# Column tiles for every product, and residual rows added by VectorE, in a recurrent-memory attention kernel

## The chip, the core and the metric

The kernel runs on one core of a Trainium2 chip, as one launch. The metric is device time in microseconds. The kernel before takes 1845.33 us (median of three runs, 1842.41 to 1847.87). Five engines work beside each other, each from its own in-order stream: TensorE (PE; the profile lists its weight loads apart, as PEld), VectorE (DVE), ScalarE (ACT), GpSimd (POOL) and SyncE (SP, which only issues DMAs here). Products are written to PSUM[...].

## What is computed

A sequence of 2048 rows of width 512 goes through two kinds of layer in turn, A, B, A, B, each with a layer norm ahead and a residual add behind.

```python
def _A_ref(x, mem0, Wq, Wk, Wv, Wo, seg_len):       # 32 heads of 128, memory of 8 rows, segments of 32
    mask = (idx[:, None] < M) | (idx[:, None] >= idx[None, :])
    mem = mem0
    for s in range(n_seg):                          # 64 segments, one after the other
        h = jnp.concatenate([mem, xs], axis=1)      # 8 + 32 rows
        q, k, v = h @ Wq, h @ Wk, h @ Wv            # (einsum per head)
        scores = where(mask, q @ k.T * scale, -1e9)
        o = softmax(scores) @ v @ Wo
        mem = o[:, :M, :].copy()                    # memory of the next segment
        outs.append(o[:, M:, :])
# B: linear attention over all rows, 32 heads of 16
    pq, pk = phi(q), phi(k)                         # phi(t) = t+1 if t>0 else exp(t), + 1e-6
    kv = sum over rows of pk x v;  z = sum of pk
    o = (pq @ kv) / (pq @ z + 1e-6) @ wo
x = x + A(layernorm(x)); x = x + B(layernorm(x))    # twice
```

Layer A is a recurrence: the projections of a segment need the memory rows that the segment before made.

## The kernel before

The kernel is written as a list of operations with what each reads and writes. A list scheduler in the kernel's own source puts them in one fixed order per engine, from rough costs and tuned priorities, and emits that with the semaphore waits that it needs.

```python
# priority of an operation: its step and a tuned offset of its name and number
nd.prio = -(step * PERIOD + OFFSET[name][k])
# on PE, the scheduler prefers to stay in the mode ("col" or "full") of the product before,
# unless another one is more urgent by MODE_SLACK
```

A segment has 40 rows. The block of 32 columns that the kernel projects as "block" holds the 8 memory rows and the first 24 rows of the segment; the remaining 8 rows of four segments ("left" rows; they don't depend on the memory for q, k and v) are projected together, once for each group G of four segments.

Projections use column tiles: four products, each with 32 stationary columns, write to the four groups of 32 PSUM partitions.

```python
for j in range(4):                                                   # L789
    r = pe.matmul(tl.f32()[32 * j:32 * j + 32, 0:512], blk[:, c, :], W[:, c, o:o + 512],
                  start=(c == 0), stop=(c == 3), tile_position=(0, 32 * j))
```

q and k are then turned, by a DMA transpose or by PE (L811), as two flags say for each half b of the heads:

```python
QDMA = (True, False)
KDMA = (True, False)
```

The memory's attention uses the whole array, with 128 stationary columns:

```python
def mm(pe, a, kk):                                                   # mem_attention
    for i, hh in enumerate(hhs):
        o = 128 * a + 32 * i
        r = pe.matmul(tl.f32()[:, o:o + 32], kk[:, hh, :, :].rearrange("p j x -> p (j x)"),   # L873
                      qT[:, r2, hh, :, 0:8], start=True, stop=True)
    return r
# once with kTl (left keys), once with kT; exp (L880); mask (L882, 128x256)
... sums: one_sb x Pm (L890, whole array); ln, exp; vimg/vleft x Pm (L903, L904, whole array)
```

The input rows have score products of their own, in column tiles, once the left queries have been copied over the memory's columns of qT:

```python
for b in range(2):                                                   # x_attention
    evac(qT[:, r2, hs, :, 0:8], qTl[:, g2, hs, :, gl], 128, ...)
    for hh in range(4 * b, 4 * b + 4):
        for j in range(4):
            r = pe.matmul(tl.f32()[32 * j:32 * j + 32, 32 * hh:32 * hh + 32], kT[:, r2, hh, j, :],   # L928
                          qT[:, r2, hh, j, :], start=True, stop=True, tile_position=(0, 32 * j))
... exp (L932), mask (L934), sums (L944, L947), scaling (L956, L958),
    vimg/vleft x Pbx (L971, L972, whole array, 128 and 32 columns)
```

The output projection (L999, column tiles) leaves its two halves on partitions 0 to 63 and 64 to 127. Copies (L609 on ACT, L610 on DVE) bring it to `outW` in 32-bit form. From there `next_mem` (L1024) makes the next memory, and for the residual a selector product sums the two halves and puts the rows in their place in a PSUM tile that is kept for four segments:

```python
def pick(pe, tl, sel, u, first, last):
    for d in range(2):
        r = pe.matmul(tl.f32()[:, 256 * d:256 * d + 256], sel(d), outW[:, u, :],              # L1041, f32r
                      start=first and d == 0, stop=last, skip_group_check=True)
# after four segments and their left rows:
add("dve", lambda v: v.tensor_tensor(x, x, tl.f32()[:, :], ALU.add), ...)                     # L1061
```

Layer B's products (L1151, L1163, L1169, L1187, L1212, L1259, L1269) and the transposes of the layer norm (L762) use the whole array. `x_move` is a DMA that GpSimd issues.

Of the kernel before, what the change touches and what calls it, by code (L numbers as in the profile page):

```python
# [6 lines left out]
F32 = mybir.dt.float32  # L7
# [12 lines left out]
MODE_SLACK = 29.57  # L20

LOOK = 0.055
# [3 lines left out]
    "ld0": (6.40,),  # L26
    "ld1": (5.00,),
    "ld2": (7.30,),
    "ld3": (-7.35,),
    "ld4": (-7.70,),  # L30
    "startF": (-6.70,),
    "prepF": (-2.85, 0.10, -2.70, 11.90, -1.50, -3.10, -1.60, 3.50, 2.40, 5.50, -13.60),
    "left0F": (0.00, 3.20, -5.50, 3.25, -0.15, 1.65, 3.95, -0.70),
    "left1F": (7.50, -11.05, 2.90, 13.75, 0.55, 0.50, 0.60, -3.30),
    "leftv0F": (-18.35, -9.35),
    "leftv1F": (-3.35, 0.00),
    "leftsF": (-2.60, 3.10, -0.60, 1.10),
    "warm": (2000.00,),
    "xlF": (7.05,),
    "qk0F": (-1.55, -16.30, 17.30, -1.50, -2.05, -2.55, -1.15, -1.55),  # L40
    "qk1F": (6.30, 1.10, -2.90, -0.20, 4.80, -6.90, 12.05, -10.25),
    "v0F": (-7.30, -21.15),
    "v1F": (33.10, -4.10),
    "mem0F": (3.95, -0.55, -1.40, -2.60, -33.00, 21.50, -6.90, -14.80, -1.80),
    "mem1F": (-1.60, 1.55, -2.50, -16.95, 7.80, -12.35, 1.60, -0.70, -1.90),
    "outF": (31.15, -14.85, 5.15, -3.10),
    "nextF": (-0.10, -1.35, -1.25),
    "xF": (-0.85, 21.45, 3.55, -11.80, -20.85, -15.05, 6.45, -1.40, 4.05, 0.30, -9.80, -5.60, -0.40, 0.95,
        1.45, 9.50, 1.00, -8.30, 8.15, 0.25, -4.40, -0.30, 0.30),
    "qk0": (-23.70, 0.00, 0.80, -6.15, 1.50, 2.10),  # L50
    "qk1": (2.90, 1.80, -13.45, 4.95, 1.10, 6.10, -0.00, -5.35),
    "v0": (1.95, -0.20),
    "v1": (10.85, -3.90),
    "mem0": (-15.05, -20.45, -14.25, -22.45, 3.65, -9.20, -4.75, 5.00, 1.60),
    "mem1": (10.75, -4.70, -1.35, -1.75, -42.80, 0.00, 11.70, -10.95, -10.30),
    "out": (-8.45, -7.05, -8.75, 2.10),
    "next": (-1.00, 6.50, -14.75),
    "res": (44.95, 1.15, -1.05, 2.95, 1.15, -20.45, -3.70),
    "x": (-2.10, 0.00, -3.10, -8.00, 2.15, -12.80, 15.20, 3.00, -3.15, -4.80, -4.50, 3.05, -0.75, -9.50, -0.40,
        0.00, -1.20, 0.05, 2.05, 4.40, 35.75, 5.95, -12.85),  # L60
    "prep": (-0.40, 0.80, 0.90, 0.75, 5.05, 11.85, 5.20, -6.20, -1.90, 12.15, -3.75),
    "left0": (-0.50, 3.85, -5.00, -2.55, -3.35, 0.30),
    "left1": (-5.30, -12.45, -0.35, -5.85, -0.70, -2.25),
    "leftv0": (39.05, 6.60),
    "leftv1": (29.85, -6.05),
    "lefts": (-7.25, 1.75, 2.50, -1.30),
    "xl": (-3.15,),
    "bi": (11.00, -1.30, -0.45, 5.25, 4.85, 6.95, -7.45, -4.85, 0.20, -18.85, -4.90, 15.35, 25.85, 0.00, 41.05,
        7.15, -0.05, -7.85, 9.60, 1.30, -1.40, 0.30, 1.25),
    "qk0L": (-16.00, 5.55, 0.60, 3.20, -1.85, -0.85, 0.10, -0.25),  # L70
    "qk1L": (-5.50, -13.55, 1.75, 1.70, -1.30, -7.25, -8.55, -2.55),
    "xL": (-0.05, -1.75, 1.75, -1.05, 4.00, 8.30, -10.35, -20.40, 3.70, 5.75, -1.75, 2.35, 1.20, -8.20, -1.65,
        4.15, -5.85, -1.65, 6.05, 0.15, -2.40),
    "lr": (-3.85, -4.35, 5.15, -13.85, -8.30, -5.75),
    "outL": (-2.55, 0.20, 1.15, 3.70),
    "resL": (-7.00, 4.00),
    "biL": (-7.30, 5.95, 1.10, -1.30, -6.60, 2.00, -0.05, 0.00, 0.00, -17.45, 2.45, 7.50, 16.85, -6.25, -3.20,
        -19.15, 19.00, 31.50, 0.25, 2.05, -0.05, -31.10, -0.35),
    "bm": (5.90, -7.40, 0.50, -3.90, 5.00, -7.20, 8.75, -4.70, 1.50, 12.25, -0.80, 20.40, 7.75),
    "boF": (0.75, 4.90, 0.00, 18.95, 10.55, 29.80, 5.70, 5.50),  # L80
    "bo": (6.95, -0.40, -16.65, -1.90, 4.25, -14.80, 4.90, 0.00),
    "ldL": (-21.30, -4.95),
    "boL": (-2.85, -30.50, 4.55, 3.30, -8.15, -12.55, 15.70),
    "boZ": (-10.55, -8.10, -4.05, 12.50, 1.95, 0.00, -4.80),
# [11 lines left out]
def c_pe4(n_mm, n):  # L96
    return n_mm / 4.0 * max(0.0255, (n / 2.4 + 3.0) * 1e-3)


def c_pe(n_mm, n):  # L100
    return n_mm * max(0.0255, (n / 2.4 + 3.0) * 1e-3)
# [24 lines left out]
class _Prog:  # L126
# [27 lines left out]
    def add(self, engs, fn, cost, reads=(), writes=(), tiles=(), dsem=None, urgent=False, mode="full",  # L154
# [337 lines left out]
def _build_kernel(nc, A_x, A_mem0, A_Wq, A_Wk, A_Wv, A_Wo, A_seg_len, B_wqkv, B_wo, out):  # L492
# [13 lines left out]
    QDMA = (True, False)  # L506
    KDMA = (True, False)
# [26 lines left out]
    selx_sb = sb("selx_sb", [128, 2, 224], F32R)  # L534
    sell_sb = sb("sell_sb", [128, 2, 128], F32R)
    selz_sb = sb("selz_sb", [128, 2, 128], F32R)
    outW = sb("outW_sb", [128, 3, 256], F32R)
    maskbd_sb = sb("maskbd_sb", [128, 128])
    epsb_sb = sb("epsb_sb", [128, 1], F32)
    eps6_sb = sb("eps6_sb", [128, 1], F32)  # L540
    memT0_sb = sb("memT0_sb", [128, 4, M])
    st_sb = sb("st_sb", [128, 2, 16], F32)


    ARENA_N = 34320
    arena = sb("arena_sb", [128, ARENA_N])
    off = [0]

# [782 lines left out]
```

The softmax here doesn't subtract the row's maximum and nothing guards it: scores larger than these inputs give would overflow.

## Time and profile before

The profiled execution lasts 1841.2 us.

| quantity | value |
|---|---|
| time, median of 3 | 1845.33 us |
| DVE busy | 1091.8 us (59%) |
| ACT busy | 1168.1 us (63%) |
| POOL busy | 76.9 us (4%) |
| mean granted TensorE clock | 0.992 |
| DMA transposes | 368, 2.9 us to landing |
| projections L789, PE busy (q, k, v) | 346.6, 318.3, 361.6 us |
| output projection L999, PE busy | 311.6 us |
| selector products L1041, PE busy | 61.4, 15.9 and 1.0 us |

How to read it: a group's busy time is the union of its instructions' times. Matmuls overlap, so the mean duration of one (381 ns for a 512-column product) is longer than the time from its start to the next start; the spacing of starts is what PE spends. In a group's line, after the bar, stand busy us and mean ns, then the idle time of the engine just before these instructions and what ended it. A shape such as 128*32 128x512 is the stationary operand (contraction by columns) and the moving one. In a line of waits stand us in total, how many, and the longest.

### The profile page before, as it was taken

How to read it: one execution, taken by the hardware profiler on the slowest of the kernel's cores; microseconds unless marked ns; L12 is line 12 of the kernel's file. 1: busy time of each engine (PE TensorE's matmuls, PEld its weight loads, DVE VectorE, ACT ScalarE, POOL GpSimd, SP SyncE). 2: the span in 40 equal slices, each digit the busy share in tenths (PEclk: the TensorE clock that was granted, in tenths of full speed). 3: DMA queues.
4: the chain of work that ended last, by engine and by line, in shares of the span. 5: the costliest groups of instructions: out<-in, count | busy, mean ns of one | idle time of the engine just before them, and what ended most of it. 6: DMA issues, size and time to landing. Idle time of an engine off the chain costs nothing.

```text
span 1841.2 us, 100785 instructions
## 1 busy us (share of the span) xinstructions
PE 1763.0 (96%) x46707; PEld 1199.6 (65%) x46707; DVE 1091.8 (59%) x3259; ACT 1168.1 (63%) x3036; POOL 76.9 (4%) x182
## 2 busy tenths in 40 slices
PE   5999999999999999999799999999999999999997
PEld 2566666666666766676566666666766766666663
DVE  2356655655666566666555655666656566666666
ACT  3566666666666666666466666666667666666664
POOL 3000000000000000000000000000000000000000
PEclk9999999999999999999899999999999999999999
DMA  9322122212222121212012222222122222122222
GB/s 366 86 35 43 38 40 38 47 38 44 38 38 41 38 46 38 42 39 41 19 26 38 40 38 49 38 41 46 38 40 47 41 43 41 41 43 48 45 74 87
DMA packets 218933, 94.85 MB, mean 52 GB/s; under 512 B 202536, under 2 KB 212656, under 8 KB 216976
## 3 DMA queue, kind: packets, MB, share of 16 engines
q1 hardware_dynamic: 211312, 60.22, 18.0%
q0 software_dynamic: 5616, 15.60, 2.9%
q10 hardware_dynamic: 1584, 12.58, 1.7%
q8 instruction: 365, 5.98, 1.4%
q14 instruction: 56, 0.46, 0.1%
HBM read 29.63 MB, written 10.49 MB: 22 GB/s over the span
## 4 chain that ended last, share of the span: by engine, by line
PE 83%; DMA 11%; ACT 3%; DVE 2%; issue 1%; SPq 0%; ACTq 0%; DVEq 0%
PE pb L789 37%; PE pb L999 16%; DMA arena_sb<-arena_sb 9%; PE pb L873 4%; PE pb L971 3%; PE pb L811 3%; PE pb L1151 3%; PE pb L1041 3%; PE pb L928 2%; PE pb L890 2%; PE pb L1187 1%; ACT arena_sb L609 1%; DMA Wk_sb<-in_A_Wk_dram 1%; PE pb L904 1%; PE pb L903 1%
## 5 line engine op out<-in xcount | busy, mean ns | idle before, releaser
L609 ACT ACTIVATE arena_sb<-pb 128x512 bf16<-128x512 f32 (+6 forms) x1365 | 674.0, 504 | 375.5 <-PE pb L789 327.8
L610 DVE CAST arena_sb<-pb 128x512 bf16<-128x512 f32 (+3 forms) x438 | 207.8, 475 | 354.3 <-PE pb L789 157.6
L789 PE MATMUL pb<-Wv_sb,arena_sb 128*32 128x512 bf16 x5120 | 361.6, 381 | 0.1
L789 PE MATMUL pb<-Wq_sb,arena_sb 128*32 128x512 bf16 x5120 | 346.6, 383 | 1.3 <-ACT arena_sb L609 0.7
L789 PE MATMUL pb<-Wk_sb,arena_sb 128*32 128x512 bf16 x5120 | 318.3, 381 | 5.5 <-DMA Wk_sb<-in_A_Wk_dram 5.5
L999 PE MATMUL pb<-Wo_sb,arena_sb 128*32 128x256 bf16 x10368 | 311.6, 274 | 4.9 <-issue 3.3
L999 PEld LDWEIGHTS pb<-Wo_sb,arena_sb 128*32 128x32 bf16 x10368 | 269.0, 97 | 16.2 <-issue 5.1
L956 DVE TENSOR_TENSOR arena_sb<-arena_sb 32x256 bf16<-32x256 bf16 x512 | 213.2, 416 | 108.6 <-ACT arena_sb L952 95.6
L789 PEld LDWEIGHTS pb<-Wk_sb,arena_sb 128*32 128x32 bf16 x5120 | 139.6, 97 | 136.5 <-DMA Wk_sb<-in_A_Wk_dram 5.7
L789 PEld LDWEIGHTS pb<-Wq_sb,arena_sb 128*32 128x32 bf16 x5120 | 134.2, 97 | 108.5 <-DVE arena_sb L610 8.8
L789 PEld LDWEIGHTS pb<-Wv_sb,arena_sb 128*32 128x32 bf16 x5120 | 136.8, 97 | 94.1 <-issue 2.8
L609 ACT ACTIVATE outW_sb<-pb 128x128 fp32r<-128x128 f32 x233 | 64.6, 277 | 171.5 <-PE pb L999 148.8
L610 DVE COPY arena_sb<-pb 128x512 bf16<-128x512 bf16 (+2 forms) x295 | 112.3, 396 | 68.6 <-PE pb L811 64.9
L971 PE MATMUL pb<-arena_sb 128*128 128x128 bf16 x1024 | 127.9, 216 | 0.0
L958 DVE TENSOR_TENSOR arena_sb<-arena_sb 32x64 bf16<-32x64 bf16 x512 | 110.8, 216 | 15.9
L873 PE MATMUL pb<-arena_sb 128*128 128x32 bf16 x2016 | 104.1, 178 | 12.4 <-DMA arena_sb<-arena_sb 11.0
L972 PE MATMUL pb<-arena_sb 128*128 128x32 bf16 x1024 | 115.0, 177 | 0.0
L880 ACT ACTIVATE arena_sb<-pb 128x256 bf16<-128x256 f32 x252 | 95.8, 381 | 27.7 <-PE pb L873 26.6
L811 PEld LDWEIGHTS pb<-id_sb,arena_sb 128*32 128x32 bf16 x4352 | 70.4, 97 | 63.7 <-ACT arena_sb L609 38.8
L811 PE MATMUL pb<-id_sb,arena_sb 128*32 128x128 bf16 x4352 | 98.0, 221 | 12.6 <-ACT arena_sb L609 7.7
L873 PEld LDWEIGHTS pb<-arena_sb 128*128 128x128 bf16 x2016 | 74.1, 96 | 52.9 <-issue 21.6
L907 DVE TENSOR_TENSOR arena_sb<-pb,arena_sb 128x128 bf16<-128x128 f32 x252 | 72.4, 288 | 42.3 <-ACT arena_sb L895 19.3
(122 smaller groups left out, 2273.7 us busy)
## 6 DMA issues: line engine op xcount, KB each, us to landing
arena_sb<-arena_sb SPq DMA_TRANSPOSE x368, 2.9
Wq_sb<-in_A_Wq_dram ACTq DMA_DIRECT2D x1, 4096.0 KB, 13.6
Wk_sb<-in_A_Wk_dram ACTq DMA_DIRECT2D x1, 4096.0 KB, 24.6
Wv_sb<-in_A_Wv_dram ACTq DMA_DIRECT2D x1, 4096.0 KB, 34.9
Wo_sb<-in_A_Wo_dram SPq DMA_DIRECT2D x4, 1024.0 KB, 11.7
xs_scratch<-x_sb POOLq DMA_DIRECT2D x32, 128.0 KB, 2.4
pq_scratch<-arena_sb POOLq DMA_DIRECT2D x32, 128.0 KB, 2.1
x_sb<-xs_scratch POOLq DMA_DIRECT2D x16, 128.0 KB, 2.6
```

The source lines that it names most:

```text
L609: return e.activation(o() if callable(o) else o, i() if callable(i) else i, ACTF.Copy)
L610: return e.tensor_copy(o() if callable(o) else o, i() if callable(i) else i)
L789: r = pe.matmul(tl.f32()[32 * j:32 * j + 32, 0:512], blk[:, c, :], W[:, c, o:o + 512], start=(c == 0), stop=(c == 3), tile_position=(0, 32 ...
L811: r = pe.transpose(tt.bf16()[32 * j:32 * j + 32, 128 * i:128 * i + 128], img[:, k, o:o + 32], id_sb[:, :], tile_position=(0, 32 * j))
L873: r = pe.matmul(tl.f32()[:, o:o + 32], kk[:, hh, :, :].rearrange("p j x -> p (j x)"), qT[:, r2, hh, :, 0:8], start=True, stop=True)
L880: add("act", lambda a: a.activation(Pm[:, k, :, :].rearrange("p a q -> p (a q)"), tl.f32()[:, 0:256], ACTF.Exp, scale=SCALE), c_act(256), ...
L907: add("dve", lambda v: v.tensor_tensor(oTb[:, s % NO, 16 * b:16 * b + 16, 0:8], pv.f32()[:, 0:128].rearrange("p (n q) -> p n q", q=8), Rm[ ...
L956: add("dve", lambda v, q=q, j=j: v.tensor_tensor(Pbx[q, :, j, 0:32], Px[q, :, :], Rx[q, :, :], ALU.mult), c_dve(256) + 0.075, reads=["Px", ...
L958: add("dve", lambda v, q=q, j=j: v.tensor_tensor(Pbx[q, :, j, 32:40], PLL[q, g2, :, gl], Rx[q, :, 0:8], ALU.mult), c_dve(64) + 0.075, read ...
L971: pe.matmul(o, vimg[:, r2, e], Pbx[:, hh, :, 0:32], start=True, stop=False)
L972: return pe.matmul(o[:, :, 0:8], vleft[:, g2, e], Pbx[:, hh, :, 32:40], start=False, stop=True)
L999: r = pe.matmul(tl.f32()[32 * j:32 * j + 32, 0:256], oT[:, 4 * hh + n, :], Wo_sb[:, 8 * n + hh, 256 * d:256 * d + 256], start=(hh == 0 and ...
```

## The change

It has four parts. The residual no longer goes through selector products, except for the last 32 rows of a layer: VectorE sums the two halves into `y_sb`, small DMAs issued by GpSimd bring the rows to their places in `dx_sb`, and one VectorE add per 128 rows brings them into x. All whole-array products become sets of four column-tile products (`quad`), so that the array can stay in one mode. The separate score products of the memory, the input and the left queries on the block's keys become one of 40 columns per head; left keys by memory queries keep one of 8 columns. And both k halves are turned by DMA, both q halves by PE. The priorities of all operations are new (numbers left out), and the scheduler's costs and constants are adapted.

```diff
-MODE_SLACK = 29.57
-LOOK = 0.055
+MODE_SLACK = 53.87
+LOOK = 0.042
... (all of OFFSET is new: before mostly within +-45, now within +-262, with a few exceptions)
-    return n_mm * max(0.0255, (n / 2.4 + 3.0) * 1e-3)
+    return n_mm * max(0.0285, (n / 2.4 + 3.0) * 1e-3)
+def quad(pe, out, lhsT, rhs, **kw):
+    for c in range(4):
+        q = slice(32 * c, 32 * c + 32)
+        r = pe.matmul(out[q], lhsT[:, q], rhs, tile_position=(0, 32 * c), **kw)
+    return r
...
-    QDMA = (True, False)
-    KDMA = (True, False)
+    QDMA = (False, False)
+    KDMA = (True, True)
...
+    NY = 2
+    y_sb = sb("y_sb", [64, NY, 256])
+    dx_sb = sb("dx_sb", [128, D])
...  mem_attention
-            def mm(pe, a, kk):
+            evac(qT[:, r2, hs, :, 32:40], qTl[:, g2, hs, :, gl], 128, ...)
+            def mm(pe, kk, n, o):
                 for i, hh in enumerate(hhs):
-                    o = 128 * a + 32 * i
-                    r = pe.matmul(tl.f32()[:, o:o + 32], kk[:, hh, :, :].rearrange("p j x -> p (j x)"),
-                                  qT[:, r2, hh, :, 0:8], start=True, stop=True)
+                    for j in range(4):
+                        r = pe.matmul(tl.f32()[32 * j:32 * j + 32, 48 * i + o:48 * i + o + n], kk[:, hh, j, :],
+                                      qT[:, r2, hh, j, 0:n], start=True, stop=True, tile_position=(0, 32 * j))
...          mm(pe, kTl[:, g2], 8, 40), then mm(pe, kT[:, r2], 40, 0); one exp of 4 x 48
-            add("dve", ... Pm, Pm, wm ... c_dve(256, 2))
+            for a in range(2):
+                add("dve", ... Pm[:, k, a, :], PQ[:, r2, b, :, 40 * a:40 * a + 8], wm ... c_dve(128))
...
-                    pe.matmul(pv.f32()[:, o], vimg[:, r2, e], Pm[:, k, 0, o], start=True, stop=False)
+                    quad(pe, pv.f32()[:, o], vimg[:, r2, e], Pm[:, k, 0, o], start=True, stop=False)
...  (the same for the other whole-array products)
...  x_attention: its score products and its exp are gone
+        def rows_out(w, tl, moves):
+            add("dve", lambda v: v.tensor_tensor(y_sb[0:64, k, :], tl.f32()[0:64, 0:256],
+                                                 outW[64:128, w, :].bitcast(F32), ALU.add), ...)
+            for i, (src, dst, n) in enumerate(moves):
+                for d in range(2):
+                    x_move(dx_sb[dst:dst + n, 256 * d:256 * d + 256],
+                           y_sb[32 * d + src:32 * d + src + n, k, :], k, ...)
...  residual
-            add("pe", lambda pe: pick(pe, tl, ... selx_sb ... w, g == 0, z), ...)
+            rows_out(w, tl, [(8, 32 * g, 24)])
...  left_rows
-            add("pe", lambda pe: pick(pe, res_tile[G], lambda d: sell_sb[:, d, :], u, False, G < NT - 1), ...)
+            rows_out(w, tl, [(8 * g, 32 * g + 24, 8) for g in range(4 if G < NT - 1 else 3)])
...
-                add("dve", lambda v: v.tensor_tensor(x, x, tl.f32()[:, :], ALU.add), ...)
+                add("dve", lambda v: v.tensor_tensor(x[0:n, :], x[0:n, :], dx_sb[0:n, :], ALU.add), ...)
```

## Prediction

> **What bounds the kernel now.** I began with the engine shares and slices of the page.
>
> ```profile
> PE 1763.0 (96%) x46707; PEld 1199.6 (65%) x46707; DVE 1091.8 (59%) x3259; ACT 1168.1 (63%) x3036; POOL 76.9 (4%) x182
> ...
> PE   5999999999999999999799999999999999999997
> ...
> PEclk9999999999999999999899999999999999999999
> ```
>
> TensorE is busy in every slice but the first, one in the middle and the last, and its clock is granted throughout. But a busy PE need not be an efficient one, so I asked next what PE waits for.
>
> ```profile
> PE pb L762 <- DVE arena_sb L756: 18.0, 5, 8.9
> PE pb L873 <- DMA arena_sb<-arena_sb: 11.0, 15, 2.2
> PE pb L811 <- ACT arena_sb L609: 7.7, 16, 0.7
> PE pb L811 <- DVE arena_sb L610: 4.8, 9, 1.1
> ```
>
> These are the long waits of PE (total us, times, longest), and they are small. L762, the largest, belongs to the start and to the two seams where a layer ends. The recurrence over segments, which could have been the limit, shows only as L873 and L811 waiting for turned q and k: about 24 us in 1841. So the kernel is bound by TensorE's own stream, and what counts is the spacing of products. I took it from the starts of successive matmuls in the trace, because their durations overlap. Medians: a set of four column-tile products takes 216 ns at 512 columns, 109 at 256, 56 at 128, 25 at 32. A product on the whole array takes 216, 56 and 25 ns at 512, 128 and 32 columns. Multiplying every kind by its count gives 1657 us. The rest of 1835 us (first to last start) is 508 changes between whole array and column tiles, and about 130 us of waits. Of these some 36 us fall before 100 us, 18 around the middle seam and 19 at the end; in between it is about 2 us in every 50.
>
> The changes are seen in the timeline (start, us, engine, line):
>
> ```profile
> 731.06 0.40 PE L811 MATMUL pb<-id_sb,arena_sb 128*32 128x128 bf16 x16
> 731.39 0.37 PE L873 MATMUL pb<-arena_sb 128*128 128x32 bf16 x8
> ...
> 720.38 0.59 PE L1151 MATMUL pb<-arena_sb 128*128 128x512 bf16 x2
> 720.90 0.38 PE L928 MATMUL pb<-arena_sb 128*32 128x32 bf16 x32
> ```
>
> The last of the sixteen L811 products takes 0.22 us and so starts at 731.24; its set would be over near 731.28; the whole-array product starts at 731.39, 0.11 us late. In the other direction the second L1151 starts near 720.60 and needs 0.216; the column product follows at 720.90, 0.09 us late. Over all pairs the lateness is 104 to 108 ns into the whole array and 81 to 94 ns out of it. I take 95 ns: 508 x 0.095 = 48 us.
>
> The groups concerned:
>
> ```profile
> L873 PE MATMUL pb<-arena_sb 128*128 128x32 bf16 x2016 | 104.1, 178 | 12.4 <-DMA arena_sb<-arena_sb 11.0 <-DVE arena_sb L610 0.8
> L1041 PE MATMUL pb<-outW_sb,selx_sb 128*128 128x256 f32 x252 | 61.4, 325 | 0.0
> L928 PE MATMUL pb<-arena_sb 128*32 128x32 bf16 x4096 | 52.1, 177 | 1.9 <-issue 1.8
> L1041 PE MATMUL pb<-outW_sb,sell_sb 128*128 128x256 f32 x64 | 15.9, 329 | 0.0
> L1041 PEld LDWEIGHTS pb<-outW_sb,selx_sb 128*128 128x128 f32 x252 | 37.7, 189 | 4.2
> ```
>
> L1041 is the residual pick. Its two products start 204 ns apart, and the next product follows the second by 122 ns: 326 ns for 512 columns in all. The 189 ns weight load of 32-bit selectors explains the first spacing.
>
> [...] Here the trace speaks against a large penalty: L928 has new weights for each of its 32 products, and its sets of four start 25 ns apart (median), like L873 on the whole array. [...]
>
> **The change, part by part.**
>
> 1. Residual. Removed: 160 pairs of f32r products, all but the last pair of each layer, so 158 x 0.326 = 51.5 us of PE. Added on VectorE: a 64x256 sum out of PSUM for each of 158 projections, about 0.42 us each (estimate between 0.29 for 128 and 0.56 for 384 elements out of PSUM, the L610 rows): 66 us. The add into x now reads SBUF instead of PSUM, 32 x (0.69 to about 0.42): 8 us less. Added on GpSimd: per layer 63 x 2 + 15 x 8 + 6 = 252, together 504 small DMAs, at 0.54 us each (the POOL rows) about 272 us of an engine that is 4% busy. They land some 2 us later (existing GpSimd moves: 2.1 to 3.1), but x is needed only once in four segments, and the last 32 rows of a layer keep the product, so this latency is off the path.
>
> 2. Column tiles for all. Whole-array products of the sums, attention products, linear-attention block and transposes become sets of four. By the spacings above their time is unchanged: 216 is 216, 56 is 56, 25 is 25. What goes is the changes of mode: 508 become about 5, -48 us. The number of matmuls grows by about 20,000, to some 66,700. About 5,400 sets of four with 64 columns or less will then exist, and L928's mean spacing was 30.5, not 25 ns. I allow 2 ns for each: +11 us.
>
> 3. Scores. Before, per segment: 16 whole-array products of 32 columns and 8 sets of 32 columns, 24 x 25 = 600 ns. After: 8 sets of 8 and 8 sets of 40 columns, 16 x 25 = 400 ns [...]. 0.2 x 128 = 26 us less. ScalarE loses one exponential per segment, 48.8 us, and some 11 us from exponentials of 192 instead of 256. VectorE has two mask products of 128 in place of one of 256: 504 of 0.2 to 0.29 us against 72 us, so +30 to +75.
>
> 4. Turning. Both k halves go by DMA and both q halves by PE, instead of q and k of half 0 by DMA: the same number of each, so no PE time. k can be projected first and its 2.9 us transfer lie beside the q projections.
>
> Sum on PE: -51.5 - 48 - 26 + 11 = -114 us. VectorE and ScalarE together go from 2260 to about 2315 us, near 1160 each in a span of 1730: 67%, not a bound. 1845 - 114 = 1731. The scheduler also no longer has to hold back urgent products to stay in a mode; for that I take off a few microseconds more and predict **1726 us**.
>
> **The rivals.**
>
> Recurrence becomes the bound. A segment takes 13.5 us now and would take 12.5. I add up its chain from rows: four projections 3.5, cast 0.6, turning and copy 0.8, scores 0.4, exponential 0.35, two masks 0.5, sums 0.3, logarithm and exponential 0.6, product 0.3, second half of the output projection 1.1, cast 0.3, memory product 0.25, copy 0.2, and about 1 for the handing over: near 10 us. That leaves 2.5 us for fillers in the wrong place, against the few waits of before. But the order of all engines is static and built anew, with much larger offsets, so a poor order can spend it: 0.3 us a segment costs 38 us, giving 1765; in a bad case nearly everything is given back.
>
> Small column sets are issue-bound. Each set is eight PE instructions in 25 ns. If long bursts run at 35 ns, 5,400 x 10 = 54 us come back: 1775. For it: the mean of L928 above its median. Against: L839 with a mean of 27.4.
>
> VectorE or the GpSimd moves delay others. The rows hold the projection's PSUM bank until VectorE has summed them. Against: a bank held for four segments becomes free, and VectorE has 30% in hand. I give this up to 20 us.
>
> It goes better: new order hides more of the remaining 2 us in 50, with 25 ns per set held: about 1695.
>
> **Range and chances.** The PE terms are measured, so their sum is trusted to about 20 us; order and bursts make the upper side longer: 1690 to 1785. Within 2% needs more than 1808, so about 80 us of the 114 lost; slower needs a new bound. Faster 0.90, same 0.06, slower 0.04.
>
> **What would show it.** Right: no whole-array products but a handful, no L1041 pairs but two, hardly any 0.1 us gaps, sets of small products at 25 to 28 ns, PE still over 95% busy and its waits as small as now; GpSimd near 20% busy with nothing waiting for it but the x add. Wrong: spacing of small sets at 35 ns or more, "issue" ahead of their weight loads, waits of PE for turned k, masks or casts of over 0.3 us a segment, or x adds waiting for row DMAs in the chain.

## The result, and the profile after

The changed kernel takes **2185.22 us** (2174.64 to 2190.19) against 1845.33: a ratio of 1.184 (95% interval 1.181 to 1.188). It was predicted at 1726, so the prediction is wrong in direction and by 459 us.

The page of the changed kernel, with the lines that answer to those of before:

```profile
PE 1748.3 (80%) x66743; PEld 1203.3 (55%) x66743; DVE 1095.5 (50%) x3369; ACT 1201.0 (55%) x3212; POOL 326.7 (15%) x660
...
PE   3788888888788888877687888788888888887786
...
PEclk9999999999999999999999999999999999999998
...
q8 instruction: 522, 8.55, 1.7%
...
PE 64%; DMA 14%; issue 13%; DVE 5%; ACT 3%; ACTq 0%; DVEq 0%
```

TensorE is still granted its clock (0.987 on the mean), yet it is busy for 80% of a longer span, idle for one to four tenths of every slice after the first. VectorE, ScalarE and GpSimd came out about as predicted; the first two are idle for nearly half the span, GpSimd for 85% of it. In the chain that ended last, "issue" now has 13%. Two lines of the page of before belong beside this:

```profile
q8 instruction: 365, 5.98, 1.4%
...
PE 83%; DMA 11%; ACT 3%; DVE 2%; issue 1%; SPq 0%; ACTq 0%; DVEq 0%
```

"Issue" is time in which the engine waited for nothing that the profile shows. The long waits of PE in the changed kernel (total us, times, longest):

```profile
PE pb L1011 <- issue: 114.2, 106, 3.6
PE pb L109 <- issue: 78.6, 77, 2.6
PE pb L887 <- DMA arena_sb<-arena_sb: 58.9, 65, 2.1
...
PE pb L796 <- DMA Wq_sb<-in_A_Wq_dram: 21.4, 1, 21.4
```

L1011 is the output projection, unchanged by the diff, L109 is `quad`, L887 the new score products, L796 the projections. All of PE's "issue" waits together are 260.5 us; before they were 6.8. Look at some in the timeline (start, us, what, and in brackets the idle time ahead):

```profile
687.23 0.61 PE L1011 MATMUL pb<-Wo_sb,arena_sb 128*32 128x256 bf16 x14
689.24 0.50 PE L1011 MATMUL pb<-Wo_sb,arena_sb 128*32 128x256 bf16 x10 [1.40 <-issue]
...
690.63 0.61 PE L1011 MATMUL pb<-Wo_sb,arena_sb 128*32 128x256 bf16 x14
692.98 0.29 PE L1011 MATMUL pb<-Wo_sb,arena_sb 128*32 128x256 bf16 x4 [1.74 <-issue]
```

TensorE stops after 14 of the 24 products that stand in a row, with the same operands, and goes on 1.4 us later. From the first restart to the second there are 10 + 48 + 8 + 48 + 14 = 128 products. That is the clue. Each product is a weight load and a matmul, so 128 products are 256 instructions. The trace gives queue q8, "instruction", 522 packets of 16,384 bytes: one packet, or block, for 256 of PE's 133,486 instructions, which makes 64 bytes each (before: 365 for 93,414). I counted PE's instructions from the start of the program and took the stalls by their place in it, modulo 256: 290 of the 522 blocks have a stall of over 0.15 us at one and the same place, together **312 us**. In the kernel before it is 17 blocks and 10.5 us. (This count, taken from start to start, is larger than that of the "issue" waits: the product ahead of a stall runs on for some 0.2 us of it, which the list of waits doesn't count as idle.)

So the theory to test is **instruction supply**: TensorE gets its instructions in blocks of 256, blocks can't follow each other faster than some interval (the shortest is 3.29 us in both traces), and where the array uses up 256 instructions sooner, it waits. Rivals: the new order (every priority changed); a cost of column tiles with new weights in the array itself; and the other three parts of the change, by the delays that they bring.

### The profile page after: what moved, and what is told of

The parts are those of the page before. It is cut to its first block, busy times and chain, and to the rows that moved or that the text cites. A ratio compares the mean times of both kernels' runs of the same rounds, so it can differ in the third digit from the quotient of the medians.

```text
span 2172.5 us, 141754 instructions
## 1 busy us (share of the span) xinstructions
PE 1748.3 (80%) x66743; PEld 1203.3 (55%) x66743; DVE 1095.5 (50%) x3369; ACT 1201.0 (55%) x3212; POOL 326.7 (15%) x660
## 4 chain that ended last, share of the span: by engine, by line
PE 64%; DMA 14%; issue 13%; DVE 5%; ACT 3%; ACTq 0%; DVEq 0%
PE pb L796 29%; PE pb L1011 14%; DMA arena_sb<-arena_sb 13%; PE pb L109 12%; PE pb L887 3%; PE pb L818 2%; DMA Wq_sb<-in_A_Wq_dram 2%; ACT arena_sb L626 1%; PE pb L1036 1%; DVE arena_sb L627 1%; DVE arena_sb L968 1%; PE pb L116 1%; ACT outW_sb L626 1%; PE pb L959 1%; DVE st_sb L756 1%
## 5 line engine op out<-in xcount | busy, mean ns | idle before, releaser
L626 ACT ACTIVATE arena_sb<-pb 128x512 bf16<-128x512 f32 (+6 forms) x1513 | 728.2, 503 | 403.2 <-PE pb L796 276.5
L109 PE MATMUL pb<-arena_sb 128*32 128x32 bf16 (+2 forms) x20416 | 401.5, 207 | 86.4 <-issue 76.2
L1011 PE MATMUL pb<-Wo_sb,arena_sb 128*32 128x256 bf16 x10368 | 366.2, 276 | 116.2 <-issue 114.2
L642 POOL DMA_DIRECT2D dx_sb<-y_sb x504 | 254.0, 510 | 1304.0 <-DVE y_sb L1048 1160.1
L796 PE MATMUL pb<-Wv_sb,arena_sb 128*32 128x512 bf16 x5120 | 372.7, 381 | 14.9 <-issue 14.9
L796 PE MATMUL pb<-Wq_sb,arena_sb 128*32 128x512 bf16 x5120 | 349.0, 385 | 27.1 <-DMA Wq_sb<-in_A_Wq_dram 21.4
L109 PEld LDWEIGHTS pb<-arena_sb 128*32 128x32 bf16 x20416 | 289.6, 95 | 140.9 <-issue 92.0
L1011 PEld LDWEIGHTS pb<-Wo_sb,arena_sb 128*32 128x32 bf16 x10368 | 272.4, 97 | 158.1 <-issue 142.2
L796 PE MATMUL pb<-Wk_sb,arena_sb 128*32 128x512 bf16 x5120 | 342.8, 381 | 12.0 <-ACT arena_sb L626 8.0
L627 DVE CAST arena_sb<-pb 128x384 bf16<-128x384 f32 (+3 forms) x329 | 175.1, 535 | 250.6 <-PE pb L109 156.6
L796 PEld LDWEIGHTS pb<-Wk_sb,arena_sb 128*32 128x32 bf16 x5120 | 156.0, 97 | 99.8 <-ACT arena_sb L626 12.2
L796 PEld LDWEIGHTS pb<-Wq_sb,arena_sb 128*32 128x32 bf16 x5120 | 146.4, 98 | 117.1 <-DMA Wq_sb<-in_A_Wq_dram 21.6
L887 PE MATMUL pb<-arena_sb 128*32 128x8 bf16 x8128 | 138.8, 174 | 81.1 <-DMA arena_sb<-arena_sb 58.9
L887 PEld LDWEIGHTS pb<-arena_sb 128*32 128x32 bf16 x8128 | 113.6, 94 | 155.0 <-DMA arena_sb<-arena_sb 69.8
L796 PEld LDWEIGHTS pb<-Wv_sb,arena_sb 128*32 128x32 bf16 x5120 | 137.0, 96 | 82.3 <-issue 25.3
L905 DVE TENSOR_TENSOR arena_sb<-arena_sb 128x128 bf16<-128x128 bf16 x504 | 98.5, 221 | 91.4 <-ACT arena_sb L898 85.7
L1048 DVE TENSOR_TENSOR y_sb<-pb,outW_sb 64x256 bf16<-64x256 f32 x158 | 65.9, 417 | 147.4 <-ACT outW_sb L626 141.4
L898 ACT ACTIVATE arena_sb<-pb 128x192 bf16<-128x192 f32 (+1 forms) x256 | 83.3, 325 | 75.9 <-PE pb L887 39.1
```

Of the source, the lines that this page charges most:

```text
L109: r = pe.matmul(out[q], lhsT[:, q], rhs, tile_position=(0, 32 * c), **kw)
L626: return e.activation(o() if callable(o) else o, i() if callable(i) else i, ACTF.Copy)
L627: return e.tensor_copy(o() if callable(o) else o, i() if callable(i) else i)
L642: add(eng, lambda e: e.dma_start(o, i), 1.1 if eng == "pool" else 0.4, reads=reads, writes=writes, dsem="%s%d" % (kind, k), lat=lat)
L887: r = pe.matmul(tl.f32()[32 * j:32 * j + 32, 48 * i + o:48 * i + o + n], kk[:, hh, j, :], qT[:, r2, hh, j, 0:n], start=True, stop=True, ti ...
L898: add("act", lambda a: a.activation(PQ[:, r2, b, :, 0:nq], tl.f32()[:, 0:192].rearrange("p (i q) -> p i q", i=4)[:, :, 0:nq], ACTF.Exp, sc ...
```

## The experiments

**The sets alone, in the order of before (b_quads).** The kernel before, its order and its mode choices kept; each bf16 whole-array product is issued as four column-tile products. The f32r picks stay whole.

```diff
-  pe.matmul(pv.f32()[:, o], vimg[:, r2, e], Pm[:, k, 0, o], start=True, stop=False)
+  quad(pe, pv.f32()[:, o], vimg[:, r2, e], Pm[:, k, 0, o], start=True, stop=False)
   ... (the same for the other bf16 whole-array products)
```

> The kernel before in its own order, with each whole-array bf16 product issued as four column-tile products (selector products stay whole); nothing else changed. PE instructions rise from 93,400 to about 142,000, blocks of 256 of them from 365 to about 555. Supply theory (PE's instructions come in blocks of 256 that follow each other at 3.3 us at the shortest, so bursts of small sets run the stream dry): 555 x 3.3 = 1830 us is the least, with more lost at block ends; 2050 us or more, over 250 us of it at block ends. Order theory (the new priorities and k by DMA made the changed kernel slow): the order here is the old one, so 1845 less some 25 us of drains, about 1820 us. Spacing theory (sets of four are slower than one whole-array product): sets start more than 25 to 28 ns apart at the median, and the loss is spread over all of them.

Measured 2349.17 us, a ratio of 1.270 (1.265 to 1.274). There are 555 blocks, and 302 of them end in a stall, 436 us in all. The median spacings are still 216, 109, 56 and 26 to 28 ns, so the sets aren't slow in the array itself. (Some of the expectations say "drain" for the 0.08 to 0.11 us of a change of mode.) PE's long waits:

```profile
PE pb L107 <- issue: 210.6, 144, 2.7
PE pb L1013 <- issue: 90.9, 73, 3.5
```

The part that the prediction counted as -48 +11 us costs about 500 by itself (2349.2 against 1849.8 for before on the same chip), with 319 of the 508 changes of mode still there, as the picks are whole. Neither the new order nor the other parts are needed for the loss.

**The change without the sets (e1_whole).**

```diff
 def quad(pe, out, lhsT, rhs, **kw):
-    for c in range(4):
-        q = slice(32 * c, 32 * c + 32)
-        r = pe.matmul(out[q], lhsT[:, q], rhs, tile_position=(0, 32 * c), **kw)
-    return r
+    return pe.matmul(out[0:128], lhsT[:, :], rhs, **kw)
```

> The changed kernel with its sets of four for sums, attention products, linear-attention block and transposes put back to one whole-array product each; residual, 40-column scores, turning and priorities stay as changed. PE instructions fall from 133,500 to about 97,000, 378 blocks. Supply theory: block-end stalls fall from 312 us to under 40, and the time to 1880 to 1930 us, in spite of some 660 changes of mode. Order theory: priorities and k by DMA are still the new ones, so it stays at 2150 us or rises with the changes of mode.

Measured 1935.99 us, 1.047 (1.043 to 1.051) of before: 249 us less than the change, and just above what was expected. It has 378 blocks, no more stalls at block ends than before has, and "issue" waits of 7.3 us. In exchange it makes 668 changes of mode where the change makes 7; 661 x 0.095 us is 63 us. 249 + 63 = 312 us, which is what the stalls at block ends added up to. That the two agree so closely is partly luck: the scheduler knows two modes again here, so the order of all engines is not that of the change. (a_quarter, below, keeps it.) Nor is it as fast as before. Its long waits are others:

```profile
PE pb L881 <- DMA arena_sb<-arena_sb: 43.5, 61, 4.0
PE pb L107 <- DVE arena_sb L899: 39.0, 63, 0.9
...
PE pb L790 <- DMA Wq_sb<-in_A_Wq_dram: 21.4, 1, 21.4
```

The score products wait for turned k, the sums for the two masks, and the first q projection for its weights. So about 86 us (1936.0 against 1849.8 on the same chip) are lost without the sets, some 15 of them to the 160 more changes of mode than before.

**Supply by itself (e3_burst).** After the end of the kernel before, products of 8 columns with nothing to wait for: first 1024 sets of four column tiles, then 2048 on the whole array.

```diff
+  for i in range(1024):
+      for j in range(4):
+          pe.matmul(tb.f32()[32 * j:32 * j + 32, 0:8], id_sb[:, 32 * j:32 * j + 32], one_sb[:, 0:8], ..., tile_position=(0, 32 * j))
+  for i in range(2048):
+      pe.matmul(tb.f32()[:, 0:8], id_sb[:, :], one_sb[:, 0:8], start=True, stop=True)
```

> The kernel before with 4096 column-tile products of 8 columns (1024 sets, 32 blocks of 256 instructions) and then 2048 whole-array products of 8 columns (16 blocks) after its last product, where nothing else runs on PE. Supply theory: after the blocks at hand are used up, blocks of the first part follow each other at about 3.3 us (103 ns per set of four instead of 25), some 100 us for the 32; the second part also needs 3.3 us a block, 25.8 ns a product, and shows almost no stalls. Spacing theory without a limit of supply: 26 us for the first part and 51 us for the second, no gaps at block ends.

The one run took 2020.6 us. The timeline of PE, at the start of the first part, in its middle, and in the second part:

```profile
1840.96 1.69 PE L1294 MATMUL pb<-one_sb,id_sb 128*32 128x8 bf16 x190 [0.78 <-DVE x_sb L1272]
1844.65 1.18 PE L1294 MATMUL pb<-one_sb,id_sb 128*32 128x8 bf16 x128 [2.00 <-issue]
...
1896.58 1.19 PE L1294 MATMUL pb<-one_sb,id_sb 128*32 128x8 bf16 x128 [2.56 <-issue]
1900.33 1.19 PE L1294 MATMUL pb<-one_sb,id_sb 128*32 128x8 bf16 x128 [2.56 <-issue]
...
1994.26 3.56 PE L1297 MATMUL pb<-one_sb,id_sb 128*128 128x8 bf16 x128 [0.47 <-issue]
```

190 products run off at once; then 128 run in 1.2 us, nothing for 2.0 to 2.8 us, 128, and so on. So what is in stock (already brought) at the start is at most some 380 instructions, one whole block and 124 of the block ahead of it. From then on a block comes every **3.74 us** (30 blocks in 112.2 us, from the first restart to the last). That is 14.6 ns per instruction, 29.2 ns per weight load with its product, 117 ns per set of four, where the array took 33. (All 32 blocks took 116.35 us; divided by 32 that is 3.64 us and 114 ns a set, figures that some of the expectations below use, but the first block and a half were in stock.) For whole-array products of 8 columns the supply is only just short: 128 products take 128 x 27 = 3.46 us, the gaps after the first are about 0.4 or 0.6, and 15 blocks from the first gap to the last take 55.9 us, 3.73 each.

The granted clock was 0.52 in the first part. But where two blocks in a row end in a stall in the changed kernel (clock 0.99), the restarts are also 3.7 us apart (3.745, the median of 176), and the fastest mean over eight blocks in a row is 3.62 us there, 3.70 in b_quads and 3.61 here, so the limit isn't the clock's. Nor is it the other DMAs': the DMA engines were busy for 2% of the first part here, for 19% of the time in the changed kernel. In the kernel before the fastest mean over eight is 4.36: it never ran into the limit for long.

That also gives a floor, as an estimate from the fastest eight: 522 blocks x 3.62 = 1890 us, whatever the order.

**The order (e4_default).** The changed kernel with all tuned priorities left out.

```diff
-OFFSET = { ... }
+OFFSET = {}
```

> The changed kernel with all tuned priorities left out: the scheduler orders by the longest remaining chain instead. The instructions are the same, only their order is not. Supply theory: the count of blocks is the same 522, so the block-end stalls stay at 200 to 400 us and the time at 2100 us or more. Order theory: the tuned numbers were what made it slow, so it changes much, to 1900 us or less.

Measured 2213.68 us, 1.197 (1.192 to 1.202), with 262 us of stalls at the ends of 214 blocks. Quite another order loses about the same. The priorities aren't the cause; the better ones gain about 1%.

**A dose (a_quarter).** The changed kernel in its order; of the attention products (sums times v) only the first of the four column tiles is issued. Three quarters of the attention outputs are left out.

```diff
+def quarter(pe, out, lhsT, rhs, **kw):
+    return pe.matmul(out[0:32], lhsT[:, 0:32], rhs, tile_position=(0, 0), **kw)
-  quad(pe, pv.f32()[:, o], vimg[:, r2, e], Pm[:, k, 0, o], start=True, stop=False)
+  quarter(pe, pv.f32()[:, o], vimg[:, r2, e], Pm[:, k, 0, o], start=True, stop=False)
   ... (and for the three other products of this kind)
```

> The changed kernel in its own order, with only the first of the four column-tile products in each set that multiplies probabilities by values (memory and input attention); the other three quarters of those outputs are left out. A single product takes the array as long as its set did, so PE's spacing and all waits stay, but 12,200 products and as many weight loads fewer are issued: 427 blocks instead of 522. Supply theory: block-end stalls fall from 312 us to under 50 and the time to 1850 to 1930 us. Order theory: nothing that an order depends on has changed, so 2185 us, within 2%. Spacing theory: these sets were the slow ones, so it falls too, but the rest of the block ends keep their stalls.

Measured 1897.81 us, 1.031 (1.026 to 1.036). In the changed kernel the products of `quad` start 5 to 8 ns after one another (medians) and its sets 26 ns (32 columns) or 56 ns (128 columns) after one another, so the four of a set run side by side. That one of them alone takes as long as its set is an estimate from this; by it the array's need hardly changes, and what is missing is instructions, 96 blocks of them. 287 us go. PE's waits:

```profile
PE pb L891 <- DMA arena_sb<-arena_sb: 58.8, 68, 3.6
...
PE pb L1015 <- issue: 19.6, 27, 1.6
PE pb L109 <- issue: 13.5, 17, 3.3
```

The wait for turned k stands as it was (58.9), the "issue" waits of L109 and the output projection fell from 192.8 to 33.1. By block ends it is 63.5 us, somewhat more than the 50 expected.

**More instructions without small sets (e2_split).** The kernel before in its order; each projection product of 512 columns becomes two of 256. Tiles, modes and order stay; by the spacings two sets of 109 ns stand in place of one of 216.

```diff
-  for j in range(4):
+  for h, j in [(h, j) for h in range(2) for j in range(4)]:
-      r = pe.matmul(tl.f32()[32 * j:32 * j + 32, 0:512], blk[:, c, :], W[:, c, o:o + 512], ...)
+      r = pe.matmul(tl.f32()[32 * j:32 * j + 32, 256 * h:256 * h + 256], blk[:, c, :],
+                    W[:, c, o + 256 * h:o + 256 * h + 256], ...)
```

> The kernel before in its own order, with each projection product of 512 columns issued as two of 256: the same array work, no column set more dense than the output projection's, but 485 blocks instead of 365. Supply theory with [...]3.6 to 3.7 us a block (replay of the old stream): 125 to 170 us more, 1975 to 2020 us, nearly all of it at block ends. Spacing theory without a limit of supply: 2 x 109 against 216 ns, 8 us more, about 1855 us.

Measured 1972.73 us, 1.071 (1.067 to 1.074), with 485 blocks and 107 us of stalls at the ends of 193 of them. The largest of PE's waits is on the split products:

```profile
PE pb L789 <- issue: 43.3, 90, 1.2
```

A set of four with 256 columns keeps the array busy for 109 ns and takes 117 to be brought (by e3_burst): with even products of this size the stock ran out at 193 block ends. Small columns aren't the cause as such; the rate of instructions is.

**Sets only in short runs (b_mixed).** The kernel before in its order, with sets in place of whole-array products only where a run of these between two runs of sets is at most 64 products long.

```diff
+  if all(r.key is not None for r in run) and not any(r.key[1][:2] in ("re", "lr") for r in run) and c.n <= 64:
+      for r in run:
+          r.sets = True
```

> The kernel before in its own order, with whole-array products issued as sets of four column tiles only where a lone run of them, at most 64 whole-array products long, stands between two runs of sets: about 60 such runs, so about 120 changes of mode fewer at 0.08 to 0.11 us each (-10 to -13 us of drains), for about 18 more blocks of instructions (383 instead of 365). Supply theory: the instruction supply has room (383 x 3.65 = 1398 us), but the replaced products stand in bursts next to sets, so some block ends stall: 10 to 25 us in all instead of 10.5; the time is 1830 to 1845 us, within 1% of before. Prediction's theory (column tiles cost nothing): 1833 us. A rival in which every set of four that stands for a whole-array product costs 114 ns: about +40 us, 1885 us.

Measured 2079.31 us, 1.129 (1.127 to 1.131), outside of all that was expected. I had misjudged how much this rule catches: about 4,500 products in 123 runs became sets, not about 60 runs, and there are 471 blocks instead of 383. 123 of 254 returns to the whole array are gone, 23 us at most, and PE's "issue" waits are 197.1 us:

```profile
PE pb L122 <- issue: 116.2, 72, 5.1
PE pb L1045 <- issue: 37.0, 34, 2.7
```

With fewer blocks than e2_split (485) it loses nearly twice as much (239 us against 130): what counts is not the number alone. A run of 64 whole-array products makes 512 instructions, which take 7.5 us to bring and, as 64 sets of 25 to 56 ns, 1.6 to 3.6 to use; a stock of some 380 instructions, as in e3_burst, can't bridge it, and long products elsewhere did not make up for it: the 471 blocks at 3.62 us would be 1705 us of the 2079.

**The picks taken away (b_nopick).** The kernel before in its order; a pick is one bf16 product of 8 columns, and x is copied instead of added to. The residual of layer A is left out.

```diff
-  for d in range(2):
-      r = pe.matmul(tl.f32()[:, 256 * d:256 * d + 256], sel(d), outW[:, u, :], ...)
+  return pe.matmul(tl.f32()[:, 0:8], id_sb[:, :], one_sb[:, 0:8], start=True, stop=True)
```

> The kernel before in its own order, with each pair of f32r selector products shrunk to one bf16 product of 8 columns, and the add of the result replaced by a copy: the residual rows of layer A are left out. The prediction's term for the selector products: 160 x (326 - 26) ns = 48 us less, 1800 us, if nothing else is waiting; if the recurrence or another wait takes its place, less than half of it comes, over 1825 us.

Measured 1827.24 us, 0.993 (0.991 to 0.995). Counted by spacings the array's need falls by 51 us, as the prediction's first step has it; the time falls by 16. PE's waits have grown, most of them small and shared with others, such as the sums' wait for the masks, of which before has 1.4 us:

```profile
PE pb L890 <- DVE arena_sb L882: 4.8, 27, 0.5
```

So a product on TensorE that is cut is worth about a third of its time here; by spacings, most of the rest came back as waits. That these are the chain of the recurrence is likely from what they wait for (turned q and k, masks), but not shown.

**The residual part alone (b_resid).** The kernel before with the first part of the change, in an order that the kernel's scheduler makes anew, with the placements of the new steps guessed. The edit, shortened:

```diff
-  pick(pe, res_tile[G], sell_sb / selx_sb, ...)             # f32r products
-  v.tensor_tensor(x, x, tl.f32()[:, :], ALU.add)
+  rows_out(w, tl, [(8, 32 * g, 24)])                        # VectorE sum, GpSimd DMAs, as in the change
+  v.tensor_tensor(x[0:n, :], x[0:n, :], dx_sb[0:n, :], ALU.add)
```

> The kernel before with the first part of the change alone: the residual rows are added by VectorE and carried by GpSimd's DMAs into dx, added to x once a group (two-set-wide products stay whole-array, score products stay at 16/16/8 columns, q and k are turned as before); seven placement values of the new steps are guessed by hand, the others are those of before. TensorE loses 157 of 158 f32r pairs (-51 us of array time) and two instructions for each of their 4 products; VectorE gets some 66 us, GpSimd about 330 us. Prediction's theory (array time is what counts): 1845 - 51 = about 1795 us. Supply theory: no stalls at ends of instruction blocks (364 blocks or fewer), so supply costs nothing, and as in the kernel with the picks cut down (-16 us) only about a third of the array time comes back: 1825 to 1840 us. Rival (the row DMAs delay x, or the guessed placements spoil the order): above 1850 us, with waits of TensorE for VectorE and for bf16 rows of xln.

Measured 1943.99 us, 1.055 (1.053 to 1.058). 363 blocks, "issue" waits of 4.8 us: supply plays no part. The changes of mode rose from 508 to 790 (282 x 0.095 = 27 us), and the other waits of PE from 65.6 to 149.8 us; VectorE waited for row DMAs only 8.7. So the expected 1825 to 1840 was wrong, and the small row waits speak for the rival of a spoiled order. How much is the order's and how much the part's own isn't separated, and the run doesn't tell what this part is worth in a good order.

**The residual part, in the order of before (b_rows).** The order is fixed first; then each pick is replaced by GpSimd DMAs that carry the rows from outW to dx in bf16 (four for a segment's 24 rows, sixteen for the left rows of a group), and two VectorE adds go directly ahead of the first reader of x. Without the change's sums on VectorE this is twice its number of DMAs, 1,008 against 504. The edit, shortened:

```diff
-  pick(pe, tl, sel, w, ...)
+  for j in range(4):
+      e.dma_start(dx_sb[dst:dst + m, h, j // 2, ...], outW[32 * j + src:32 * j + src + m, w, :])   # on pool
-  v.tensor_tensor(x, x, tl.f32()[:, :], ALU.add)
+  for k in range(2): v.tensor_tensor(x[0:n, :], x[0:n, :], dx_sb[0:n, h, k, :], ALU.add)
```

> The kernel before in its own order, with the first part of the change done after the order is fixed: each f32r pick but the last is replaced by four GpSimd DMAs that carry the rows from outW into dx (rounded to bf16 on the way), and the one VectorE add of a group by two adds of 128x512 from dx, put directly ahead of the first reader of x. Nothing else moves: the other instructions keep their order, and no placement is guessed. TensorE loses 157 pairs (-51 us of array time) and some 130 changes of mode (-12 us); VectorE gets some 30 us, GpSimd some 330 us. If the part's own merit is what the kernel with cut-down picks showed (-16 us, a third of the array time) plus the same share of the drains: 1818 to 1830 us against 1840, a ratio of 0.989 to 0.995. If the +100 us of the part alone under a new order came from the part itself (rows that come late, VectorE and GpSimd in each other's way), it comes back here too: 1880 us or more, with waits for dx or for bf16 rows of xln. If it came from the order, it does not.

Measured 2120.86 us, 1.151 (1.149 to 1.154): the expectation's "1880 us or more", with rows that come late. First a wait of VectorE, then one of PE, in this kernel:

```profile
DVE x_sb L1149 <- DMA dx_sb<-outW_sb: 211.1, 30, 8.0
```

```profile
PE pb L893 <- ACT arena_sb L702: 247.5, 39, 8.8
```

In the order of before, the last rows of a group are picked just ahead of the layer norm that reads x. A pick gives them in 0.4 us. Here 9 to 20 DMAs stand in a row on GpSimd ahead of the long waits, at 0.507 us each, and the add starts 1.1 us after the last is issued: VectorE waits 7 us on average at 30 adds, and PE, behind it in its fixed order, about as long. The changed kernel has no such wait: its 504 DMAs and their adds have room, and VectorE waits 0.4 us for rows in all. In this form the part needs an order that leaves it some 8 us; the change's own form with half the DMAs wasn't tried in the order of before.

**A cheaper pick (b_bf16), and picks as sets where they stand alone (b_bf16c).** The kernel before in its order. outW and the selectors are kept in bf16, so that a pick moves 256 columns in 109 ns instead of 204; in the second kernel, whole-array runs that consist of picks alone become sets of four.

```diff
-  selx_sb = sb("selx_sb", [128, 2, 224], F32R)
-  outW = sb("outW_sb", [128, 3, 256], F32R)
+  selx_sb = sb("selx_sb", [128, 2, 224], BF16)
+  outW = sb("outW_sb", [128, 3, 256], BF16)              # also sell, selz, selm
 # b_bf16c alone:
-  r = pe.matmul(tl.f32()[:, 256 * d:256 * d + 256], sel(d), outW[:, u, :], ...)
+  r = quad(pe, tl.f32()[:, 256 * d:256 * d + 256], sel(d), outW[:, u, :], ...)
```

> The kernel before in its own order with the projected rows outW and the selectors kept in bf16 instead of f32r: the picks stay on TensorE, as bf16 products of 256 columns at 109 ns instead of f32r ones at 204 ns, so 316 products x 95 ns = -30 us of array time, with the same number of instructions (365 blocks, no stalls by supply). If two thirds of a saving on TensorE go into other waits, as with the picks cut down to 8 columns (-51 us of array time, -16 us of time): about -10 us, 1830 to 1837 us against 1842. Prediction's theory (array time is what counts): 1812 us. Nothing is left out; the rows that are added to x are rounded to bf16 first.

> As the kernel with bf16 picks, and where a run of whole-array products between two runs of sets consists of picks alone (about 68 places), these are issued as sets of four column tiles: some 136 changes of mode fewer at 0.08 to 0.11 us (-11 to -15 us of drains), for some 68 x 12 = 820 more instructions, 3 more blocks (368). A pick set moves 256 columns and keeps the array busy for 109 ns, against 114 ns of supply for a set of four, so the buffer is hardly drawn on: stalls at ends of blocks within 10 us of before's. Expected: a further 4 to 12 us off, 1822 to 1832 us. If drains were hidden in waits anyway: no difference from the kernel with bf16 picks.

Measured 1835.94 us, 0.9985 (0.9975 to 0.9995), and 1826.61 us, 0.993 (0.992 to 0.995). The second beats both kernels. The groups of its picks:

```profile
L119 PE MATMUL pb<-outW_sb,selx_sb 128*128 128x256 bf16 x178 | 33.7, 270 | 0.0
...
L122 PE MATMUL pb<-outW_sb,selx_sb 128*32 128x256 bf16 x296 | 15.4, 271 | 0.0
L122 PE MATMUL pb<-outW_sb,sell_sb 128*32 128x256 bf16 x240 | 12.0, 273 | 0.0
```

The cheaper pick saves about 3 us (0.9 to 4.6 by the interval). The 30 us of array time that I expected it to cut were counted wrongly: only the first product of a pair had been followed after 204 ns, the second after 122, so it is 158 x (0.326 - 0.218) = 17 us, and a sixth of that comes back. (That it saved instructions too I had missed: in 32-bit form the memory product was issued twice for each bf16 one, 2,016 against 1,008 records, so 357 blocks, not 365.) The 134 sets add 402 products and 3 blocks and take away 134 changes of mode, and 9 us come back of 134 x 0.095 = 13. Here the idea of the change works: the sets are few, 256 columns long and far from one another, and the stalls at block ends have not grown (some 12 us in both kernels, counted by weight loads, since 80 matmul records are missing from this trace).

## Why the prediction was wrong

The step that failed is the second: "By the spacings above their time is unchanged", with its only reserve, "I allow 2 ns for each: +11 us". What the runs put in its place is 312 us of stalls at block ends in the changed kernel, and about 500 us in the kernel that makes this step alone.

The working was not wrong about the array. By count times median spacing, with each change of mode at 0.095 us, it needs 1697 us before and 1573 after, 124 us less where the sum said 114: medians are still 216, 109, 56 and 25 ns, and 7 changes of mode are left. The mistake was to take the median spacing inside bursts as a rate that can be kept up. L928, the proof that small sets run at 25 ns, has 32 products in a burst, 64 instructions; the burst of e3_burst found some 380 in stock. So the burst of L928 showed the array and not the supply: in e3_burst sets take 33 ns while a block lasts and 117 over many blocks (granted clock 0.52).

The prediction did name the rival, "Small column sets are issue-bound", and its sign, "issue" ahead of weight loads. It sized it by a guess on the spacing (10 ns for 5,400 sets, 54 us), and looked for it in these sets' own spacing. The stalls instead fall wherever a block happens to end, 114 us of them on the output projection, which hadn't been touched. The page of before held the number: 365 packets on q8. With 20,000 more products the count of blocks becomes 522, and the shortest interval between two such packets in the trace of before is 3.29 us: 522 x 3.29 = 1717 us, nearly all of the predicted time, before a single stretch is unbalanced.

Point by point otherwise:

- Residual. The pieces were right: 65.9 us of VectorE sums (66 predicted), 0.43 us adds out of `dx_sb` (0.69 out of PSUM before), 254 us of GpSimd DMAs (272), nothing waiting for the rows. That 51.5 us of array time are 51.5 us of time isn't borne out: with the picks cut down in the kernel before, only 16 of 51 came back.
- Scores and ScalarE. Sets of 40 columns start 25 ns apart in the trace (median), as the count had them. VectorE and ScalarE came to 2296 us together (2315 predicted). But the masks now have PE waiting, 19 us against 2 (stalls counted by spacing).
- Turning. "so no PE time" left out the waits: PE waits 67 us for turned k, 13 before, about 0.5 us a segment, which the prediction had named as a sign of being wrong. Not part of the turning, but of the new kernel: 21.4 us once at the start for Wq, the first weights to be needed (at 35.4 us, Wk at 42.2), which it loads last and before loaded first.
- "Recurrence becomes the bound" was given 2.5 us a segment of room. b_nopick speaks for the room being in use already: two thirds of what TensorE saves turn into waits.

So the gain of 124 us was made in the array, and PE's waits and stalls (the rest of the time from the first start to the last) grew from 138 to 592 us: by some 302 at block ends (10.5 to 312) and by some 152 of other kinds. 454 less 124 is 330 us, and the profiled executions differ by 331 (1841.2 and 2172.5). How these 152 divide between part 4, the masks, the late Wq, and an order made for other costs stays open. Parts 3 and 4 weren't tried alone, and b_resid, 104 us slower with part 1 in a new, unadjusted order, shows how little a part tried like that would tell.

What the runs show of the supply is this: stalls begin after about 380 instructions (e3_burst), and where 256 instructions after 256 take the array less than about 3.7 us, it waits (3.74 us a block in e3_burst, 3.745 in the changed kernel). The cost of a change of mode held: 0.08 to 0.11 us in the trace of before, and b_bf16c, where 134 changes fewer gave 9 us.

## What to carry to other kernels

Before splitting products, count instructions. In the changed kernel the 522 packets of queue q8 (all PE's) times 3.62 us, the fastest mean over eight, make 1890 us, more than the 1726 predicted; and where the array used up block after block of 256 PE instructions (128 products) in less than 3.62 to 3.74 us, it was left standing, 312 us in all. In these runs column-tile sets in place of whole-array products paid once (b_bf16c, 9 us), where they were few, 256 columns long and far from one another; trading one 25 ns whole-array product for a set takes 117 ns of supply in place of 29 (e3_burst), to save a 0.1 us change of mode that a whole run of products shares. And the spacing of a burst is to be held against the stock before it is used as a rate: L928's burst is 64 instructions, the stock in e3_burst was some 380.

## What the hardware showed unexpectedly

- Where nothing else held TensorE up, a block of 256 instructions came every 3.74 us, 14.6 ns each, weight loads counted, at a granted clock of 0.52 (e3_burst), and every 3.745 us (median) at 0.99 (the changed kernel). At the fastest over eight blocks it was 3.61 and 3.62. A packet itself takes 1.05 us (median) before and 1.07 after, so most of the interval isn't the transfer.
- In the changed kernel 290 of 522 blocks have their stall at one place modulo 256 in program order, on whatever product stands there, as "issue".
- A whole-array product of 8 columns every 27 ns was slightly faster than the supply in e3_burst: with the gaps it was one in 29.1 ns.
- A 32-bit product of the memory step is two pairs of weight load and matmul where a bf16 one is one (2,016 records before, 1,008 in b_bf16): 1,008 pairs and 8 blocks less for one type changed.
